# The first group of a causal dynamic convolution and squared-ReLU MLP kernel: turned blocks, raw weight loads, unread products and the third group's first pieces

## The chip, the cores and the metric

The kernel runs on one core of a Trainium2 chip. The core's engines are TensorE (PE in the profile), VectorE (DVE), ScalarE (ACT), GpSimd (POOL) and SyncE (SP), which here issues every transfer; each takes its own instructions in order, and semaphores tie them together. The metric is the device time of one execution in microseconds (us), the median of three runs.

## The reference

```python
# _attn_ref: x is 4 x 4096 x 192, weight_gen 4 x 4096 x 8 heads x 7 taps
w = weight_gen - np.max(weight_gen, axis=-1, keepdims=True)
w = np.exp(w)
w = w / (np.sum(w, axis=-1, keepdims=True) + 1e-09)
pad = K - 1
x_pad = np.concatenate([np.zeros((B, pad, D), dtype=np.float32), x], axis=1)
idx = np.arange(S)[:, None] + np.arange(K)[None, :]
x_unf = x_pad[:, idx, :]
x_unf = x_unf.reshape(B, S, K, H, group)
out = np.einsum('bshk,bskhg->bshg', w, x_unf)
# _moe_ref: w_in is 192 x 2048, w_out 2048 x 192, s and b scalars
h = x @ w_in
r = np.maximum(h, 0.0)
g = s * (r * r) + b
return (g @ w_out).astype(np.float32)
```

A softmax over seven taps weights, for each token and each head of 24 channels, the token and the six before it; the 16384 rows of 192 channels that come out go through an MLP of width 2048. The two weight matrices arrive in double precision; the kernel reads them as pairs of 32-bit words.

## The kernel before

**Tiling.** The tokens are cut into 32 groups of 512. The width of 2048 is cut into four quads of 512, and each quad into two chunks of 256: eight chunks, numbered 0 to 7. Products that must be exact to float32 are made from a high and a low part of each operand: xa and xb hold the high and low parts of the first 128 and the other 64 channels, `wc` of a chunk those of w_in and w_out, gh and gl those of the hidden layer.

**The raw words.** `load_weights(k)` fetches two chunks of w_in and w_out into one tile `r`: four loads of 32 partitions (L183), eight small ones for the channels beyond 32 of each block of 48, called tails here (L194), then w_out by chunk (L201). `convert(i)` turns chunk i into `wc` in four steps that the program places one at a time with `ahead`: the absolute value on ACT (L215); the bits of the high part on DVE (L218 to L226); the high part's cast on ACT (L231) and the low word on DVE (L233, L237); six matmuls and a cast that make the low part (L247 to L250).

**The first group** goes chunk by chunk in the loop at L682, beside the conversion: the first product (`mm1_pair`, L512 and L518), relu and square on ACT (`relu2`, L548 to L554, the last being gh), gl on DVE (`low_g`, L572), the second product of the chunk before (`mm2_pair`, L599). Between them stand pieces of the second group's convolution (`run_pieces(1, ...)`: softmax L297 to L314 with the exponent L305 on ACT, products L329, sums L340 and after). The first group's own convolution (`first_pieces`) is in another layout: x in one tile of 128 partitions, products L411, sums L422 and L433, then 16 matmuls that turn the blocks (`turn`, L446), a cast for the high part (L454) and a difference for the low part (L459). At the last chunk `column_sums` adds the columns of w_out on PE (L274) into a PSUM tile, and `set_bias` reads it on DVE (L282, L283).

**The other groups** run by quads in the loop at L709 (`mm1_quad` L537, `mm2_quad` L617), with the convolution of the group after next to them, `scale` (L629, L635) and `store` (L645 to L654; the last group's are at L651).

**What sets the order.** The program order is the order of each engine (`manual_schedule`); nothing reorders it. Tiles of one tag in a pool take turns in their buffers, so a write waits for the readers of the tile before. SP issues all transfers in order, and their completions go round eight semaphores: the issue of a transfer waits until the transfer eight places before it has landed.

## Time and profile before

| | us |
|---|---|
| median of three runs | 1170.17 |
| lowest and highest of them | 1169.68, 1171.65 |
| the profiled execution | 1168.92 |
| its span, first to last instruction | 1167.2 |
| PE busy in the span | 1138.5 (98%) |
| DVE busy | 937.7 (80%) |
| ACT busy | 824.0 (71%) |

The profile is of one execution. Busy time is summed over an engine's instructions; an idle stretch is put down to what ended it. A microsecond of DVE, ACT or DMA matters only where the engine that sets the end waits for it, so the waits of PE and the chain that ended last are read ahead of the shares.

### The profile page before, as it was taken

Reading aid. Unit: us, or ns where it says so; the run is one execution under the profiler, and the core shown is the slowest. Engines: PE = TensorE matmul, PEld = TensorE weight load, DVE = VectorE, ACT = ScalarE, POOL = GpSimd, SP = SyncE. Lnnn points to the kernel's source line nnn. Section 1 sums busy time; section 2 is a strip of 40 time slices with the busy share of each in tenths; the row PEclk is TensorE's granted clock in tenths of the full one; section 3 lists DMA queues with packets and bytes.
Section 4 is the critical chain, followed back from the end, with each engine's and each line's share of the span. In section 5 each row is a group of like instructions: output and inputs, shape, how many; then the busy total and the mean of one; then the engine's idle time right before and its main releaser. Section 6 shows DMA issues by size and latency. Waiting matters only on the chain.

```text
span 1167.2 us, 29890 instructions
## 1 busy us (share of the span) xinstructions
PE 1138.5 (98%) x12688; PEld 1033.1 (89%) x12688; DVE 937.7 (80%) x1354; ACT 824.0 (71%) x887; POOL 6.2 (1%) x24
## 2 busy tenths in 40 slices
PE   2999999999999999999999999999999999999998
PEld 2688999999999999999999999999999999999997
DVE  7888887788987777887778888778898777888854
ACT  2767767777677677676776776777767777777674
POOL 0000000000000000000000000000000000000000
PEclk9999999999999999999999999999999999999999
DMA  6421222221122221122222122222112222212110
GB/s 159 122 44 29 39 46 47 33 47 25 37 47 47 36 44 33 33 43 47 46 33 47 25 37 46 47 33 46 28 34 46 47 38 42 35 35 39 24 24 14
DMA packets 171145, 50.35 MB, mean 43 GB/s; under 512 B 160196, under 2 KB 163908, under 8 KB 171012
## 3 DMA queue, kind: packets, MB, share of 16 engines
q1 hardware_dynamic: 171012, 48.45, 22.2%
q8 instruction: 99, 1.62, 0.6%
q14 instruction: 34, 0.28, 0.1%
HBM read 27.70 MB, written 12.58 MB: 35 GB/s over the span
## 4 chain that ended last, share of the span: by engine, by line
PE 96%; DVE 2%; DMA 1%; SPq 0%; ACT 0%; issue 0%
PE po L617 48%; PE ph L537 43%; PE po L599 2%; PE ph L512 1%; PE ph L247 1%; PE ph L518 1%; DMA x<-in_x_dram 0%; DVE pr L422 0%; PE ph L446 0%; DVE gl L572 0%; SPq L194 0%; PE ph L274 0%; ACT gh L554 0%; PE ph L249 0%; PE ph L248 0%
## 5 line engine op out<-in xcount | busy, mean ns | idle before, releaser
L617 PE MATMUL po<-wc,gh 64*128 64x384 f32 x3936 | 575.8, 355 | 0.0
L617 PE MATMUL po<-wc,gl 64*128 64x192 f32 x3936 | 475.9, 249 | 0.9 <-DVE gl L572 0.9
L572 DVE TENSOR_TENSOR gl<-r,gh 128x1024 fp32r<-128x1024 f32 x256 | 312.9, 1222 | 199.8 <-ACT gh L554 194.4
L548 ACT ACTIVATE r<-ph 128x1024 f32<-128x1024 f32 x254 | 247.1, 1023 | 290.4 <-PE ph L537 283.8
L617 PEld LDWEIGHTS po<-wc,gl 64*128 64x128 f32 x3936 | 373.3, 187 | 5.9 <-DVE gl L572 1.1
L617 PEld LDWEIGHTS po<-wc,gh 64*128 64x128 f32 x3936 | 369.2, 184 | 4.8
L537 PE MATMUL ph<-xa,wc 64*128 64x512 f32 x2976 | 359.4, 387 | 0.0
L537 PEld LDWEIGHTS ph<-xa,wc 64*128 64x128 f32 x2976 | 278.2, 185 | 50.4 <-issue 0.2
L554 ACT CAST gh<-r 128x1024 fp32r<-128x1024 f32 x254 | 267.1, 1051 | 7.8
L550 ACT ACTIVATE r<-r 128x1024 f32<-128x1024 f32 x254 | 268.6, 1058 | 0.3
L537 PE MATMUL ph<-xb,wc 64*128 64x512 f32 x1488 | 189.0, 386 | 0.0
L329 DVE TENSOR_TENSOR pr<-xt,w 128x1536 f32<-128x1536 f32 (+1 forms) x124 | 187.5, 1553 | 1.4 <-DVE w L314 0.2
L537 PEld LDWEIGHTS ph<-xb,wc 64*128 64x128 f32 x1488 | 139.6, 184 | 29.1
L340 DVE TENSOR_TENSOR pr<-pr 128x1536 f32<-128x1536 f32 (+1 forms) x124 | 140.7, 1155 | 2.1
L629 DVE SCALAR_TENSOR_TENSOR u<-po,s_sb,bias 128x192 f32<-128x192 f32 x128 | 49.7, 409 | 2.1 <-PE po L599 2.1
L635 DVE SCALAR_TENSOR_TENSOR y<-po,s_sb,u 128x192 f32<-128x192 f32 x128 | 49.7, 408 | 0.1
L348 DVE TENSOR_TENSOR acc<-pr 128x768 f32<-128x768 f32 x31 | 29.7, 958 | 1.1
L247 PE MATMUL ph<-r,eye_f 128*128 128x384 f32 x32 | 15.4, 566 | 15.3 <-DVE r L226 15.3
L359 DVE STREAM_TRANSPOSE xT<-acc 128x128 f32<-128x128 f32 x124 | 27.6, 280 | 1.0
L364 DVE STREAM_TRANSPOSE xT<-acc 128x128 f32<-128x128 f32 x124 | 26.3, 269 | 0.0
L599 PE MATMUL po<-wc,gh 128*128 128x384 f32 x80 | 23.7, 361 | 0.0
L247 PEld LDWEIGHTS ph<-r,eye_f 128*128 128x128 f32 x32 | 5.8, 204 | 18.1 <-issue 18.1
(59 smaller groups left out, 360.5 us busy)
## 6 DMA issues: line engine op xcount, KB each, us to landing
xt<-in_x_dram SPq DMA_DIRECT2D x120, 132.0 KB, 3.4
out_dram<-y SPq DMA_DIRECT2D x124, 96.0 KB, 1.9
xb<-xb SPq DMA_DIRECT2D x124, 64.0 KB, 2.3
wg<-in_weight_gen_dram SPq DMA_DIRECT2D x124, 28.0 KB, 2.6
r<-in_moe_w_out_dram SPq DMA_DIRECT2D x8, 384.0 KB, 3.6
r<-in_moe_w_in_dram SPq DMA_DIRECT2D x12, 128.0 KB, 2.6
x<-in_x_dram SPq DMA_DIRECT2D x1, 960.0 KB, 5.3
r<-in_moe_w_in_dram SPq DMA_DIRECT2D x24, 32.0 KB, 1.9
```

What stands on the lines that cost most here:

```text
L247: nc.tensor.matmul(out=o, lhsT=eye_f, rhs=fv[:, c], start=True, stop=False)
L329: nc.vector.tensor_tensor(out=pr[:, k0:k1, :, h * G:(h + 1) * G], in0=bass.AP(xs.tensor, xs.offset, [xs.ap[0], [FQ, n], [FQ, J], [1, G]]), ...
L340: nc.vector.tensor_tensor(out=pr[:, o:o + n], in0=pr[:, o:o + n], in1=pr[:, a:a + n], op=ALU.add)
L537: nc.tensor.matmul(out=h_t[n, p][:, j], lhsT=w1(2 * k + p, part, block, j, rows), rhs=v[rows], start=(at < 2 and c == 0), stop=(at >= 4 an ...
L548: nc.scalar.activation(out=r[p], in_=h_t.pop((n, p)), func=AF.Relu)
L550: nc.scalar.activation(out=r[p], in_=r[p], func=AF.Square)
L554: nc.scalar.copy(out=gh, in_=r[p])
L572: nc.vector.tensor_tensor(out=gl, in0=sq, in1=gh.bitcast(F32), op=ALU.subtract)
L599: nc.tensor.matmul(**m)
L617: nc.tensor.matmul(**m)
L629: nc.vector.scalar_tensor_tensor(out=u[i], in0=o_t[g][tiles[i]][:, 1, :], scalar=s_sb, in1=bias, op0=ALU.mult, op1=ALU.add,)
L635: nc.vector.scalar_tensor_tensor(out=y[:, t], in0=o_t[g][t][:, 0, :], scalar=s_sb, in1=u[i - 1], op0=ALU.mult, op1=ALU.add,)
```

## The change

The change has six parts. The first group's x is loaded in two transfers, cut after the seventh token's words of each partition. The raw words of w_in come in one transfer a chunk, of 128 partitions, in place of four of 32 for one or two chunks; w_out's chunk follows it directly, ahead of the tails, on the same queue. The blocks are turned into two PSUM tiles, h1 and one of the output tiles, in place of the two halves of h0, so the output tiles are now whole banks. `keep_warm` issues seven and, later, four matmuls on x0 whose result nobody reads. For chunk 0 the low cast of chunk 1 stands ahead of the square, and gl ahead of the second group's softmax. And at the last chunk the third group's softmax and first product stand ahead of gl and of `set_bias`; the pieces and `scale` in the next two quads are cut accordingly.

```diff
@@ -138,10 +138,11 @@
             in_=wgf[t0:t0 + T].rearrange("(p t) n -> p (t n)", t=NT),
         )
         src = xf[t0 - HALO:t0 - HALO + 1, 0:1]
-        nc.sync.dma_start(
-            out=x0.rearrange("p t d -> p (t d)"),
-            in_=bass.AP(src.tensor, src.offset, [[NT * D, P], [1, (NT + HALO) * D]]),
-        )
+        for a, b in ((0, K * D), (K * D, (NT + HALO) * D)):
+            nc.sync.dma_start(
+                out=x0.rearrange("p t d -> p (t d)")[:, a:b],
+                in_=bass.AP(src.tensor, src.offset + a, [[NT * D, P], [1, b - a]]),
+            )
         xt_t[0], wg_t[0] = x0, wg
 
     def zeros_before(i):
@@ -170,38 +171,45 @@
     w_in_u = w_in.bitcast(U32)
     w_out_u = w_out.bitcast(U32)
 
-    def load_weights(k, chunks=(slice(0, 2),)):
+    def raw_tile(k):
 
         if k not in raw_t:
             raw_t[k] = raw.tile([P, 2, CW, 2], U32, tag="r", name="r")
-        rw = raw_t[k].rearrange("p c n w -> p c (n w)")
-        for cs in chunks:
-            n = cs.stop - cs.start
-            c0 = (k * QUAD + cs.start * 2) * P * 2
-            src = w_in_u[0:1, c0:c0 + 1]
-            for q in range(Q):
+        return raw_t[k].rearrange("p c n w -> p c (n w)")
+
+    def load_chunk(i):
+
+        k, c = divmod(i, 2)
+        rw = raw_tile(k)
+        src = w_in_u[0:1, i * 4 * P:i * 4 * P + 1]
+        nc.sync.dma_start(
+            out=rw[:, c, CA * 2:CB * 2],
+            in_=bass.AP(src.tensor, src.offset, [[FQ * F * 2, Q], [F * 2, 32], [1, 4 * P]]),
+        )
+        src = w_out_u[i * 2 * P:i * 2 * P + 1, 0:1]
+        nc.sync.dma_start(
+            out=rw[:, c, CO * 2:].rearrange("p (j n) -> p j n", j=2),
+            in_=bass.AP(src.tensor, src.offset, [[D * 2, P], [P * D * 2, 2], [1, D * 2]]),
+        )
+
+    def load_tails(k, c0, n):
+
+        rw = raw_tile(k)
+        for q in range(Q):
+            for i in range(2):
+                f = (q + 2 * i) % Q * FQ + 32
+                c = (k * QUAD + c0 * 2 + 1 - q // 2) * P * 2
+                src = w_in_u[f:f + 1, c:c + 1]
                 nc.sync.dma_start(
-                    out=rw[q * 32:(q + 1) * 32, cs, CA * 2:CB * 2],
-                    in_=bass.AP(
-                        src.tensor, src.offset + q * FQ * F * 2, [[F * 2, 32], [2 * P * 2, n], [1, 2 * P * 2]]
-                    ),
-                )
-            for q in range(Q):
-                for i in range(2):
-                    f = (q + 2 * i) % Q * FQ + 32
-                    c = c0 + (1 - q // 2) * P * 2
-                    src = w_in_u[f:f + 1, c:c + 1]
-                    nc.sync.dma_start(
-                        out=rw[q * 32 + i * TAIL:q * 32 + (i + 1) * TAIL, cs, CB * 2:CO * 2],
-                        in_=bass.AP(src.tensor, src.offset, [[F * 2, TAIL], [2 * P * 2, n], [1, P * 2]]),
-                    )
-            for c in range(cs.start, cs.stop):
-                o = (k * 2 + c) * 2 * P
-                src = w_out_u[o:o + 1, 0:1]
-                nc.sync.dma_start(
-                    out=rw[:, c, CO * 2:].rearrange("p (j n) -> p j n", j=2),
-                    in_=bass.AP(src.tensor, src.offset, [[D * 2, P], [P * D * 2, 2], [1, D * 2]]),
-                )
+                    out=rw[q * 32 + i * TAIL:q * 32 + (i + 1) * TAIL, c0:c0 + n, CB * 2:CO * 2],
+                    in_=bass.AP(src.tensor, src.offset, [[F * 2, TAIL], [2 * P * 2, n], [1, P * 2]]),
+                )
+
+    def load_weights(k):
+
+        for i in (2 * k, 2 * k + 1):
+            load_chunk(i)
+        load_tails(k, 0, 2)
 
     def convert(i):
 
@@ -440,24 +448,25 @@
 
         def turn():
             pr = st["v"]
-            st["ph"] = ph = ps_h.tile([P, 2, T], F32, tag="h0", name="ph")
+            ph = ps_h.tile([P, 2, T], F32, tag="h1", name="ph")
+            st["ph"] = ph[:, 0], ps_o.tile([P, T], F32, tag="o0", name="po")
             for a in range(2):
                 for t in range(NT):
                     nc.tensor.matmul(
-                        out=ph[:, a, t * P:(t + 1) * P], lhsT=pr[:, 3 + a, t * P:(t + 1) * P], rhs=eye_f,
+                        out=st["ph"][a][:, t * P:(t + 1) * P], lhsT=pr[:, 3 + a, t * P:(t + 1) * P], rhs=eye_f,
                         start=True, stop=True,
                     )
 
         def split_hi():
             st["x"] = x = [xtp.tile([P, 2, T], F32R, tag=n, name=n) for n in ("xa", "xb")]
             for h in range(2):
-                nc.scalar.copy(out=x[h][:, 0], in_=st["ph"][:, h])
+                nc.scalar.copy(out=x[h][:, 0], in_=st["ph"][h])
 
         def split_lo():
             x = st["x"]
             for h in range(2):
                 nc.vector.tensor_tensor(
-                    out=x[h][:, 1], in0=st["ph"][:, h], in1=x[h][:, 0].bitcast(F32), op=ALU.subtract
+                    out=x[h][:, 1], in0=st["ph"][h], in1=x[h][:, 0].bitcast(F32), op=ALU.subtract
                 )
             x_t[0] = [[(0, v[:, 0]), (1, v[:, 0]), (0, v[:, 1])] for v in x]
 
@@ -466,6 +475,13 @@
             add(0, 3, 2), add(2, 5), add(2, 6), add(0, 1), last_add,
             turn, split_hi, split_lo,
         ]
+
+    def keep_warm(n):
+
+        o = ps_o.tile([P, T], F32, tag="o1", name="po")
+        x0 = xt_t[0].rearrange("p t d -> p (t d)")[:, 0:2 * D]
+        for _ in range(n):
+            nc.tensor.matmul(out=o[:, 0:2 * D], lhsT=eye_f, rhs=x0, start=True, stop=True)
 
     pieces_t = {}
 
@@ -541,14 +557,16 @@
             if at < 2:
                 hand_over(h_t[n, at])
 
-    def relu2(n, ps=(0, 1), between=None):
+    def relu2(n, ps=(0, 1), between=None, early=False):
         r = {}
         for p in ps:
             r[p] = act.tile([P, 2, T], F32, tag="r", name="r")
             nc.scalar.activation(out=r[p], in_=h_t.pop((n, p)), func=AF.Relu)
         for p in ps:
+            if between and early:
+                between()
             nc.scalar.activation(out=r[p], in_=r[p], func=AF.Square)
-            if between:
+            if between and not early:
                 between()
             gh = gp.tile([P, 2, T], F32R, tag="gh", name="gh")
             nc.scalar.copy(out=gh, in_=r[p])
@@ -573,7 +591,8 @@
         g_t[n, p] = gh, gl
 
     def outputs(g):
-        o_t[g] = [ps_o.tile([P, 2, D], F32, tag=f"o{t}", name="po") for t in range(NT)]
+        banks = [ps_o.tile([P, T], F32, tag=f"o{t}", name="po") for t in range(NT)]
+        o_t[g] = [o[:, 0:2 * D].rearrange("p (a d) -> p a d", a=2) for o in banks]
         y_t[g] = yp.tile([P, NT, D], F32, tag="y", name="y")
 
     def second(n, p, j, t, part, rows=slice(0, P)):
@@ -656,7 +675,9 @@
     with tc.manual_schedule():
         load_first()
         constants()
-        load_weights(0, (slice(0, 1), slice(1, 2)))
+        for i in range(2):
+            load_chunk(i)
+            load_tails(0, i, 1)
         load(1)
         load_weights(1)
         nc.sync.dma_start(out=s_sb, in_=s.partition_broadcast(P))
@@ -669,10 +690,11 @@
                 next(parts[i])
 
         run_pieces(0, 0, 2)
+        keep_warm(7)
         ahead(0, 1)
-        run_pieces(0, 2, 5)
-        run_pieces(0, 5, 7)
+        run_pieces(0, 2, 7)
         ahead(0, 3)
+        keep_warm(4)
         ahead(1, 1)
         run_pieces(0, 7, 14)
         ahead(1, 1)
@@ -685,7 +707,7 @@
             if i == 0:
                 ahead(1, 1)
                 ahead(2, 1)
-            relu2(n, [p], lambda: ahead(i + 1, 1))
+            relu2(n, [p], lambda: ahead(i + 1, 1), i == 0)
             if i == 0:
                 run_pieces(1, 0, 2)
             ahead(i + 2, 2)
@@ -694,8 +716,13 @@
                 sums = column_sums()
             if i > 0:
                 mm2_pair((i - 1) // 2, (i - 1) % 2)
+            if i == 0:
+                low_g(n, p)
             run_pieces(1, *beside[i])
-            low_g(n, p)
+            if i == NC - 1:
+                run_pieces(2, 0, 4)
+            if i > 0:
+                low_g(n, p)
             if i == 0:
                 load_weights(2)
             if i == NC - 1:
@@ -704,7 +731,7 @@
                 load_weights(3)
             if i == 4:
                 load(2)
-        run_pieces(2, 0, 3)
+        run_pieces(2, 4, 5)
         last = NG * NQ - 1
         for n in range(NQ, last + 1):
             g, k = divmod(n, NQ)
@@ -723,10 +750,13 @@
             else:
                 mm2_quad(n - 1)
             a = (3, 5), (5, 8), (9, 14), (0, 2)
-            run_pieces(g + 1 + k // 3, *a[k])
+            a = {NQ: (5, 7), NQ + 1: (7, 8)}.get(n, a[k])
+            run_pieces(g + 1 + k // 3, *a)
+            if n == NQ:
+                scale(g - 1, (0, 2))
             low_g(n, 0)
             if k == 0:
-                scale(g - 1, (0, 2, 1, 3))
+                scale(g - 1, (1, 3) if n == NQ else (0, 2, 1, 3))
                 store(g - 1, 0, NT)
             low_g(n, 1)
             a = (5, 5), (8, 9), (14, 15), (2, 3)
```

**SP, the raw words of chunks 2 and 3.** The rows are transfers by line, written tile and shape; `r` is the tile of raw words, DMAHW0 to DMAHW7 are the eight completion semaphores. Before (the first two loads of 32 partitions stand just ahead):

```order
L183 DMA r<-in_moe_w_in_dram 32x2x512 [waits DMAHW6_49]
L183 DMA r<-in_moe_w_in_dram 32x2x512 [waits DMAHW7_49]
L194 DMA r<-in_moe_w_in_dram 16x2x256 [waits DMAHW0_49]
L194 DMA r<-in_moe_w_in_dram 16x2x256 [waits DMAHW1_49]
L194 DMA r<-in_moe_w_in_dram 16x2x256 [waits DMAHW2_49]
L194 DMA r<-in_moe_w_in_dram 16x2x256 [waits DMAHW3_49]
L194 DMA r<-in_moe_w_in_dram 16x2x256 [waits DMAHW4_49]
L194 DMA r<-in_moe_w_in_dram 16x2x256 [waits DMAHW5_49]
L194 DMA r<-in_moe_w_in_dram 16x2x256 [waits DMAHW6_49]
L194 DMA r<-in_moe_w_in_dram 16x2x256 [waits DMAHW7_49]
L201 DMA r<-in_moe_w_out_dram 128x2x384 [waits DMAHW0_49]
L201 DMA r<-in_moe_w_out_dram 128x2x384 [waits DMAHW1_49]
```

Now:

```order
L185 DMA r<-in_moe_w_in_dram 128x1x512 [waits DMAHW7_49]
L190 DMA r<-in_moe_w_out_dram 128x2x384 [waits DMAHW0_49]
L185 DMA r<-in_moe_w_in_dram 128x1x512 [waits DMAHW1_49]
L190 DMA r<-in_moe_w_out_dram 128x2x384 [waits DMAHW2_49]
L203 DMA r<-in_moe_w_in_dram 16x2x256 [waits DMAHW3_49]
L203 DMA r<-in_moe_w_in_dram 16x2x256 [waits DMAHW4_49]
L203 DMA r<-in_moe_w_in_dram 16x2x256 [waits DMAHW5_49]
L203 DMA r<-in_moe_w_in_dram 16x2x256 [waits DMAHW6_49]
L203 DMA r<-in_moe_w_in_dram 16x2x256 [waits DMAHW7_49]
L203 DMA r<-in_moe_w_in_dram 16x2x256 [waits DMAHW0_49]
L203 DMA r<-in_moe_w_in_dram 16x2x256 [waits DMAHW1_49]
L203 DMA r<-in_moe_w_in_dram 16x2x256 [waits DMAHW2_49]
```

Two loads of 128 partitions, each with w_out behind it, now stand ahead of the tails; before, w_out came after them. The last tail waited for DMAHW7, that of the fourth w_in load; it now waits for the semaphore of the second w_out.

**ACT, the first chunk.** The absolute value (of chunk 2's raw words), relu, square, low cast of chunk 1 (`wc_105`), gh and the exponent. Before:

```order
L215 ACTIVATE t<-r 128x768
L548 ACTIVATE r<-ph 128x1024
L550 ACTIVATE r<-r 128x1024
L250 CAST wc_105<-ph 128x768
L554 CAST gh<-r 128x1024
L305 ACTIVATE e<-e 128x224
```

Now:

```order
L223 ACTIVATE t<-r 128x768
L564 ACTIVATE r<-ph 128x1024
L258 CAST wc_105<-ph 128x768
L568 ACTIVATE r<-r 128x1024
L572 CAST gh<-r 128x1024
L313 ACTIVATE e<-e 128x224
```

The low cast of chunk 1 and the square have changed places; the absolute value of chunk 2 stands ahead of the relu in both.

**DVE, the end of the first group.** Low parts of xb and xa of the second group, gl of the last chunk, the two reads of the column sums (`cs`, `bias`), and the third group's softmax and products. Before:

```order
L377 TENSOR_TENSOR xb<-xT,xb 128x512
L377 TENSOR_TENSOR xa<-xT,xa 128x512
L572 TENSOR_TENSOR gl<-r,gh 128x1024
L282 TENSOR_SCALAR cs<-ph,b_sb 128x192
L283 SCALAR_TENSOR_TENSOR bias<-ph,b_sb,cs 128x192
L297 TENSOR_REDUCE mx<-wg 128x32
L299 TENSOR_TENSOR e<-wg,mx 128x224
L310 TENSOR_REDUCE sm<-e 128x32
L311 TENSOR_SCALAR sm<-sm 128x32
L312 RECIPROCAL sm<-sm 128x32
L314 TENSOR_TENSOR w<-e,sm 128x224
L329 TENSOR_TENSOR pr<-xt,w 128x64x24 x2
```

Now:

```order
L385 TENSOR_TENSOR xb<-xT,xb 128x512
L385 TENSOR_TENSOR xa<-xT,xa 128x512
L305 TENSOR_REDUCE mx<-wg 128x32
L307 TENSOR_TENSOR e<-wg,mx 128x224
L318 TENSOR_REDUCE sm<-e 128x32
L319 TENSOR_SCALAR sm<-sm 128x32
L320 RECIPROCAL sm<-sm 128x32
L322 TENSOR_TENSOR w<-e,sm 128x224
L337 TENSOR_TENSOR pr<-xt,w 128x64x24
L590 TENSOR_TENSOR gl<-r,gh 128x1024
L290 TENSOR_SCALAR cs<-ph,b_sb 128x192
L291 SCALAR_TENSOR_TENSOR bias<-ph,b_sb,cs 128x192
```

The softmax and one product, which stood behind the reads of the column sums, stand ahead of gl and of these reads.

## Rows read from the trace of the kernel before

**Rows 1.** The page: the chain that ended last; the first weight product.

```profile
PE 96%; DVE 2%; DMA 1%; SPq 0%; ACT 0%; issue 0%
...
L247 PE MATMUL ph<-r,eye_f 128*128 128x384 f32 x32 | 15.4, 566 | 15.3 <-DVE r L226 15.3
```

**Rows 2.** Waits of PE, 0 to 130 us: total, times, longest.

```profile
PE ph L446 <- DVE pr L433: 2.9, 1, 2.9
PE ph L512 <- DVE xb L459: 2.6, 1, 2.6
...
PE po L617 <- DVE gl L572: 0.9, 1, 0.9
```

**Rows 3.** Stretches: length, busy time by engine, granted clock, DMA share, GB/s.

```profile
21.90:25.30 3.40, 3.36 (x16) 3.37 (x16) 2.71 (x6) 0.00 (x0) 0.00 (x0) 0.50 1.04 225
...
28.70:32.10 3.40, 3.40 (x12) 1.81 (x10) 3.04 (x6) 0.91 (x1) 0.00 (x0) 0.50 0.40 135
...
33.05:40.00 6.95, 6.30 (x27) 3.80 (x25) 4.46 (x8) 6.77 (x10) 0.00 (x0) 1.00 0.37 108
...
100.00:1167.00 1067.00, 1061.63 (x12260) 973.62 (x12258) 855.14 (x1237) 764.96 (x821) 5.32 (x16) 1.00 0.21 38
```

**Rows 4.** Timeline, DVE and PE at chunk 3: start, duration, line, tiles.

```profile
53.53 1.22 DVE L572 TENSOR_TENSOR gl<-r,gh 128x1024 fp32r<-128x1024 f32 x1
...
54.80 0.36 PE L599 MATMUL po<-wc,gl 128*128 128x192 f32 x1
```

**Rows 5.** Timeline, PE: the first product of chunk 0 and of chunk 2.

```profile
28.14 2.42 PE L512 MATMUL ph<-xa,wc 128*128 128x512 f32 x6 [2.58 <-DVE xb L459]
...
43.10 1.56 PE L512 MATMUL ph<-xa,wc 128*128 128x512 f32 x6
```

**Rows 6.** The page: transfers, size of one, median us to landing.

```profile
xt<-in_x_dram SPq DMA_DIRECT2D x120, 132.0 KB, 3.4
...
x<-in_x_dram SPq DMA_DIRECT2D x1, 960.0 KB, 5.3
r<-in_moe_w_in_dram SPq DMA_DIRECT2D x24, 32.0 KB, 1.9
```

**Rows 7.** Timeline, ACT: chunk 2's absolute value, chunk 0's relu.

```profile
29.49 0.91 ACT L215 ACTIVATE t<-r 128x768 f32<-128x768 f32 x1 [2.03 <-DVE v L237]
32.18 1.02 ACT L548 ACTIVATE r<-ph 128x1024 f32<-128x1024 f32 x1 [1.78 <-PE ph L518]
```

**Rows 8.** Stretches as in rows 3: the x load, the last stores.

```profile
3.50:5.00 1.50, 0.00 (x0) 0.00 (x0) 0.97 (x4) 0.39 (x1) 0.00 (x0) 1.00 1.01 420
...
1162.00:1165.00 3.00, 0.00 (x0) 0.00 (x0) 0.50 (x2) 0.00 (x0) 0.00 (x0) 1.00 0.27 87
```

**Rows 9.** Timeline, SP: the second group's x loads are issued.

```profile
18.13 2.30 SPq L125 DMA_DIRECT2D xt<-in_x_dram  x4
```

**Rows 10.** Timeline, DVE: from chunk 2's conversion to chunk 3's.

```profile
33.21 0.96 DVE L237 SCALAR_TENSOR_TENSOR v<-r,t 128x768 fp32r<-128x768 uint32 x1
36.48 0.39 DVE L310 TENSOR_REDUCE sm<-e 128x32 f32<-128x224 f32 x1 [2.31 <-ACT e L305]
...
37.93 1.76 DVE L329 TENSOR_TENSOR pr<-xt,w 128x1536 f32<-128x1536 f32 x1
39.61 1.22 DVE L572 TENSOR_TENSOR gl<-r,gh 128x1024 fp32r<-128x1024 f32 x1
40.74 0.55 DVE L218 TENSOR_SCALAR t<-t 128x768 f32<-128x768 f32 x1
```

**Rows 11.** Timeline, all engines: the end of the first group.

```profile
82.12 1.05 ACT L554 CAST gh<-r 128x1024 fp32r<-128x1024 f32 x1
...
83.20 1.22 DVE L572 TENSOR_TENSOR gl<-r,gh 128x1024 fp32r<-128x1024 f32 x1 [3.64 <-ACT gh L554]
...
84.34 0.41 DVE L282 TENSOR_SCALAR cs<-ph,b_sb 128x192 f32<-128x192 f32 x1
...
85.10 3.03 PE L537 MATMUL ph<-xa,wc 64*128 64x512 f32 x24
...
85.96 0.39 ACT L305 ACTIVATE e<-e 128x224 f32<-128x224 f32 x1 [2.79 <-DVE e L299]
```

## The prediction

> **What bounds the kernel now.** I read the chain that ended last first. Its row says that PE holds 96% of the span [rows 1], so a microsecond counts only where PE stands still, or where it will after the change. The list of PE's waits says where that is. Three of its rows bear on the change: the blocks of the first group wait 2.9 us for DVE (L446), the first product of the MLP 2.6 us for the last low part (L512 after L459), and L617 0.9 us for a low part of g at the end of the first group [rows 2]. The stretches come next: from 100 us to the end PE is busy in all but half a percent of the time at a granted clock of 1.00, and the list of waits has nothing there, so whatever the first 90 us lose or gain passes one for one to the end [rows 3]. The rest of the reading asks what sets the pace of those 90 us. There PE and DVE are tied: in the fourth chunk DVE ends gl at 53.53 + 1.22 = 54.75, and PE's product with it starts at 54.80 [rows 4]. A delay of DVE in that stage is a delay of PE.
>
> The clock is the last thing to see. In the two stretches that follow the waits of 2.9 and 2.6 us the granted clock was 0.50, the lower of the two levels; after 33.05 us it is 1.00 [rows 3]. The same six matmuls of L512 took 2.42 us there and 1.56 us later [rows 5], so a stretch of 3.4 us at the lower level, as both were, costs 3.4 x (1 - 1.56/2.42) = 1.2 us.
>
> **The front: x in two loads, turned blocks in two tiles, eleven unread products.** The x load took 5.3 us [rows 6]; the second part is 576 of 1920 words, so the first product starts at most 30% of that, 1.6 us, earlier. The separate tiles take the second half of the turning out of the wait for xa: up to the 2.6 us of that wait go. The unread products are of the size of L247, 0.57 us each [rows 1]. Seven take 4.0 us inside the 15.3 us that PE waits for the first conversion, and are free. Four more take 2.3 us of the wait of 2.9; if the blocks are ready sooner than I think, they hold PE up to 2.3 us. What they may buy is the higher clock, up to 2 x 1.2 us. All of this makes the first product of the MLP early, by 2 to 5 us. It is not what is late next.
>
> **What is late next: the raw words of chunks 2 and 3.** ACT takes its work in order, and L215 of chunk 2 stands ahead of the relu of chunk 0; before, it ran at 29.49 and the relu at 32.18 [rows 7]. Queued behind it now are that relu, the low cast of chunk 1, the square, gh and the exponent of the second group's weights; DVE's gl and conversion and PE's second product wait for them. L215 needs the last of eight tails. Eight semaphores go round, so each transfer's issue waits until the one eight places before it has landed. With one w_in load a chunk and w_out ahead of the tails, the fifth to eighth tails wait for w_in 2, w_out 2, w_in 3 and w_out 3.
>
> How long do these take? The source of the new w_in load has 4 as its slowest dimension. The nearest row is that of the last stores (L651), whose destination has 4 there too: the share of the 16 DMA engines was 0.27, four of 16, at 87 GB/s, where the x load had all of them and 420 [rows 8]. So I take 256 KB (262 thousand bytes) at 87 GB/s, 3.0 us; the best that four engines can do by the x load's row is 420/4 = 105 GB/s, 2.5 us. The 393 thousand bytes of w_out take 0.9 us at 420. They are behind one another on those four engines: 2 x (3.0 + 0.9) = 7.8 us. They begin when the second group's x is through. Its loads are issued by 18.13 + 2.30 = 20.43 [rows 9] and land 3.4 us later [rows 6]: 23.8. So w_out 3 lands at 31.6, the eighth tail is issued then and lands after 1.9 [rows 6], at 33.5, and L215 runs at 33.6 where it ran at 29.49: 4.1 us late.
>
> That row is of a store, this is a load. The Trainium skill ("DMA: Bandwidth & Descriptors", section "Why a DMA increments its semaphore by 16 and not by 1") says that the number of engines is the largest up to 16 that divides the slowest dimension of both sides, and it makes no difference between loads and stores. By that rule this load has four; the trace of before agrees for the store with its 0.27. Were it sixteen, the sum would be that of the first rival.
>
> From there by DVE and ACT. Relu at 33.6 + 0.9 = 34.5 (L215 takes 0.91); relu 1.02, the low cast some 0.8, square and gh some 1.05 each: gh is there at 38.4. DVE's conversion of chunk 2 ended at 33.21 + 0.96 = 34.17, 4.7 after L215 began, so now at 38.3 [rows 7, 10]. Then gl, moved ahead of the pieces, 1.22 (39.6); the softmax of the second group, 37.93 - 36.48 = 1.45 (41.05); its first product, 39.61 - 37.93 = 1.68 (42.7). Chunk 3's conversion starts there; before it started at 40.74 [rows 10]. That is **+2.0 us** in a chain without slack [rows 4]. Moving gl ahead of the pieces takes away PE's 0.9 at 40 us, but it does not shorten DVE's row of work, and the row is what counts. The ends: with 2.5 us a load, +1.0; with a last tail that takes as long as the x loads (3.4 for 1.9), +3.5. Less than nothing is the first rival.
>
> **The end of the first group: the third group's pieces ahead of the last low part.** PE's seventh matmul of the next group's first product (at wc_105) writes the tile that holds the column sums, so it waits for set_bias, two reads on DVE. Before, gl(7) started at 83.20, right behind gh (82.12 + 1.05), took 1.14 and was followed by the reads, 84.34 to 85.2; PE came to that matmul at 85.10 + 6 x 0.126 = 85.86 and did not wait [rows 11]. Now DVE runs the maximum and difference (in its idle 3.64 us, free), then waits for the exponent, which stands behind gh on ACT: 83.17 + 0.39 = 83.56. Then softmax 1.45, the product 1.68, gl 1.14, the reads 2 x 0.41 [rows 10, 11]: 88.65. PE waits 88.65 - 85.86 = **+2.8 us**. Behind that matmul on PE stand all later ones, so nothing covers it. What is bought is the wait of 0.9 at L617 [rows 2], since DVE has less to do behind set_bias: **-0.9**. Both ends are narrow (exponent overlapping gh, -0.1).
>
> A wait of 2.8 us is as long as the two (2.9 and 2.6) that were followed by the lower clock [rows 2, 3]. I take one stretch of it, **+1.2**, at 5 in 7; without it the sum is 1.2 less. The pieces and the scale that are cut differently in the fifth and sixth quads move DVE work within a stretch where PE had no waits [rows 3]; I put them at nothing, since PE would have to wait there first.
>
> **Sum.** +2.0 + 2.8 - 0.9 + 1.2 = +5.1 on the profiled 1168.92: 1174.0. The profiled run is 1.25 below the median of three, 1170.17, so the median becomes 1175.3. Ends of the forecast: +1.0 + 2.8 - 0.9 = +2.9 (1173.1) and +3.5 + 2.8 + 1.2 = +7.5 (1177.7).
>
> **Rivals.** *Sixteen engines.* If the w_in load is spread after all, chunks 2 and 3 (1.5 MB) take some 3.7 us at 420 GB/s from 23.8, and with the tail L215 runs at about 29.4, as before. Then the early first product counts: relu at 30.2, gh at 34.1, DVE 34.2 + 1.22 + 1.45 + 1.68 = 38.55 instead of 40.74, -2.2. With the end of the group, -2.2 + 2.8 - 0.9 = -0.3, or +0.9 with the clock: 1169.9 to 1171.1, no change. For it: the tile's side has 128 partitions, and no load of this shape is in the trace; against it, the store's row. *The front carries.* Before, L215 of chunk 2 was released by DVE, not by a transfer [rows 7]; it waited for the conversion behind the turned blocks. Those come earlier by up to the 1.6 us of the x load and part of the 2.6 us of PE's wait, some 3 us in all, and if the words of chunks 2 and 3 are in by then, L215 goes at 26.5 and DVE gains 2.2 + 3 = 5.2: -5.2 + 2.8 - 0.9 = -3.3, 1166.9. It is faster by over 0.2% from a gain of 4.2 on, with L215 at 27.3 or sooner. Against it: even sixteen engines bring the words only at about 29, by the reckoning above, unless SP's issues move up by 2 us. *Four engines, but PE keeps its clock* is the forecast less 1.2: 1174.1.
>
> **How the numbers follow.** What a measurement of this kernel can tell from no change is about 0.2%, 2.3 us: 1167.8 to 1172.5. The forecast has 0.74 (0.53 with the lower clock, 0.21 without, all of it slower). Sixteen engines has 0.18, of which 0.15 is within and 0.03, with less gained at the front, slower. The front carries has 0.08, faster. So faster 0.08, same 0.15, slower 0.77. The range reaches down to the first rival's lower end, 1170.0, and up to the forecast's upper end, rounded up, 1178.0; outside are the second rival and some 0.08 above.
>
> **What would show it.** In the changed kernel's trace: the w_in load alone on the queue at a DMA share near 0.25 and some 3 us; L223 (the old L215) of chunk 2 at 33 to 34, released by a DMA; chunk 3's conversion on DVE at 42 to 43; a wait of PE at L553 for DVE L291 of 2.5 to 3 us near 88, and a granted clock of 0.5 behind it; no wait at L636. I am wrong if L223 of chunk 2 runs by 30, if the wait at L553 is under 1.5 us, or if PE shows a slack to DVE in the middle chunks that takes up the 2.0.

## The result and the profile after

The changed kernel takes 1176.47 us (median of six runs, 1175.98 to 1177.29) where the kernel before takes 1170.31 beside it: ratio 1.0051, 95% interval 1.0038 to 1.0064, slower by 6.2 us. The profiled execution took 1176.62 us with a span of 1174.9, against 1168.92 and 1167.2: 7.7 us more, which the trace has to account for. Each column of the table is one execution; that of before lies 1.4 us under the median of its kernel, that of after 0.15 above.

| start, us | before | after | later by |
|---|---|---|---|
| SP: x loads of the second group | 18.13 | 20.77 | 2.64 |
| ACT: absolute value of chunk 2 | 29.49 | 36.20 | 6.71 |
| DVE: conversion of chunk 3 | 40.74 | 45.03 | 4.29 |
| ACT: relu of chunk 7 | 79.97 | 84.32 | 4.35 |
| PE: first quad of the next group | 85.10 | 89.46 | 4.36 |
| PE: second quad | 91.88 | 100.80 | 8.92 |
| PE: third quad | 101.86 | 109.57 | 7.71 |

After the third quad nothing is gained or lost. So there are three places: 4.36 us by the first quad, 8.92 - 4.36 = 4.56 between it and the second, and 1.21 given back by the third.

The waits of PE over the whole span (total, times, longest) answer to [rows 2]:

```profile
PE ph L528 <- ACT r L564: 8.1, 1, 8.1
...
PE ph L553 <- DVE bias L291: 2.7, 1, 2.7
PE ph L528 <- DVE xa L468: 0.8, 1, 0.8
```

The 2.9 at the turned blocks and the 0.9 at the third group's second product are gone, and of the 2.6 at the first product of the MLP 0.8 is left. The second chunk's product (L528) now waits 8.1 us for the relu of chunk 0, and the next group's first product (L553) 2.7 us for the second read of the column sums. Why the relu is late stands on ACT (timeline: start, duration, line, idle before and its releaser; answers to [rows 7]):

```profile
36.20 0.89 ACT L223 ACTIVATE t<-r 128x768 f32<-128x768 f32 x1 [10.36 <-DMA r<-in_moe_w_in_dram]
36.99 1.01 ACT L564 ACTIVATE r<-ph 128x1024 f32<-128x1024 f32 x1
```

ACT stood idle for 10.4 us until a tail of w_in had landed, with the relu behind it. SP's timeline shows what the tails themselves waited for; the four rows of L203 are the fifth to eighth tails of chunks 2 and 3, each issued when w_in 2, w_out 2, w_in 3 and w_out 3 had landed (answers to [rows 9]):

```profile
20.77 2.29 SPq L125 DMA_DIRECT2D xt<-in_x_dram  x4
...
29.82 0.31 SPq L203 DMA_DIRECT2D r<-in_moe_w_in_dram  x1
...
30.76 0.31 SPq L203 DMA_DIRECT2D r<-in_moe_w_in_dram  x1
...
33.33 0.31 SPq L203 DMA_DIRECT2D r<-in_moe_w_in_dram  x1
...
34.26 0.31 SPq L203 DMA_DIRECT2D r<-in_moe_w_in_dram  x1
```

From w_out 2 to w_in 3 there are 2.57 us, from w_in 2 to w_out 2 and from w_in 3 to w_out 3 0.94 and 0.93. In a stretch between, with the w_in load almost alone, the DMA share was 0.26 (last but one number; the clock stands ahead of it), as for the last stores in [rows 8]:

```profile
32.00:33.00 1.00, 0.00 (x0) 0.00 (x0) 0.00 (x0) 0.00 (x0) 0.00 (x0) 0.98 0.26 97
```

Behind the wait of 8.1 us PE's granted clock was 0.50. This did not add to the delay: DVE, whose row of work the chunks follow, had no gap from chunk 2's conversion (37.12) to chunk 3's (45.03).

```profile
38.00:42.00 4.00, 3.95 (x10) 2.53 (x12) 3.90 (x6) 3.97 (x6) 0.00 (x0) 0.50 0.85 209
```

The end of the first group, all engines (answers to [rows 11]):

```profile
87.43 0.38 ACT L313 ACTIVATE e<-e 128x224 f32<-128x224 f32 x1
87.84 0.39 DVE L318 TENSOR_REDUCE sm<-e 128x32 f32<-128x224 f32 x1 [3.21 <-ACT e L313]
...
89.29 1.76 DVE L337 TENSOR_TENSOR pr<-xt,w 128x1536 f32<-128x1536 f32 x1
89.46 0.96 PE L553 MATMUL ph<-xa,wc 64*128 64x512 f32 x6
90.97 1.22 DVE L590 TENSOR_TENSOR gl<-r,gh 128x1024 fp32r<-128x1024 f32 x1
92.10 0.41 DVE L290 TENSOR_SCALAR cs<-ph,b_sb 128x192 f32<-128x192 f32 x1
92.55 0.42 DVE L291 SCALAR_TENSOR_TENSOR bias<-ph,b_sb,cs 128x192 f32<-128x192 f32 x1
...
93.12 3.14 PE L553 MATMUL ph<-xa,wc 64*128 64x512 f32 x18 [2.70 <-DVE bias L291]
```

Softmax, product, gl and the reads stand in a row, and PE, after six matmuls, waits for the last of them. In the stretches behind that wait (granted clock third from the end) the clock is at its lower level, 0.50, from 95 to 97, and back at 1.00 from about 98.5; the first two rows mix both levels:

```profile
93.00:96.50 3.50, 3.38 (x22) 3.19 (x24) 3.50 (x3) 0.00 (x0) 0.00 (x0) 0.70 0.03 5
96.50:98.50 2.00, 2.00 (x13) 1.54 (x10) 0.67 (x1) 0.93 (x2) 0.00 (x0) 0.67 0.00 0
98.50:100.80 2.30, 2.30 (x16) 2.14 (x16) 0.88 (x3) 2.27 (x4) 0.00 (x0) 1.00 0.00 0
...
95.00:97.00 2.00, 2.00 (x12) 1.84 (x12) 2.00 (x2) 0.00 (x0) 0.00 (x0) 0.50 0.04 8
```

4.56 - 2.70 = 1.86 us is therefore what follows the wait in this execution. Most of it is the clock, but not all: with the same wait and no lower clock behind it (128 rows, pieces alone) the time between the two quads is still 0.25 us longer than before and the wait together.

### The profile page after: what moved, and what is told of

Read it like the earlier page. It is cut to its first block, busy times and chain, and to the rows that moved or that the text cites. A ratio compares the mean times of both kernels' runs of the same rounds, so it can differ in the third digit from the quotient of the medians.

```text
span 1174.9 us, 29916 instructions
## 1 busy us (share of the span) xinstructions
PE 1148.4 (98%) x12710; PEld 1039.3 (88%) x12710; DVE 938.0 (80%) x1354; ACT 823.6 (70%) x887; POOL 6.1 (1%) x24
## 4 chain that ended last, share of the span: by engine, by line
PE 96%; DMA 2%; SPq 1%; DVE 0%; ACT 0%; issue 0%; ACTq 0%
PE po L636 48%; PE ph L553 43%; DMA r<-in_moe_w_out_dram 2%; PE po L618 2%; PE ph L528 1%; PE ph L255 1%; PE ph L534 1%; SPq L105 0%; SPq L185 0%; SPq L125 0%; PE ph L257 0%; PE ph L256 0%; ACT r L564 0%; DVE pr L337 0%; DMA r<-in_moe_w_in_dram 0%
## 5 line engine op out<-in xcount | busy, mean ns | idle before, releaser
L553 PE MATMUL ph<-xa,wc 64*128 64x512 f32 x2976 | 360.4, 388 | 2.7 <-DVE bias L291 2.7
L553 PEld LDWEIGHTS ph<-xa,wc 64*128 64x128 f32 x2976 | 279.3, 185 | 52.9 <-issue 3.4
L553 PE MATMUL ph<-xb,wc 64*128 64x512 f32 x1488 | 189.9, 388 | 0.0
L553 PEld LDWEIGHTS ph<-xb,wc 64*128 64x128 f32 x1488 | 140.8, 185 | 28.9
L367 DVE STREAM_TRANSPOSE xT<-acc 128x128 f32<-128x128 f32 x124 | 27.6, 280 | 1.0
L223 ACT ACTIVATE t<-r 128x768 f32<-128x768 f32 x8 | 7.3, 908 | 23.0 <-DMA r<-in_moe_w_in_dram 23.0
L528 PE MATMUL ph<-xa,wc 128*128 128x512 f32 x48 | 14.6, 439 | 8.9 <-ACT r L564 8.1
```

What stands on the lines that cost most here:

```text
L553: nc.tensor.matmul(out=h_t[n, p][:, j], lhsT=w1(2 * k + p, part, block, j, rows), rhs=v[rows], start=(at < 2 and c == 0), stop=(at >= 4 an ...
```

## The experiments

Every time is set against the kernel before on the same chip in the same session; those medians lie between 1169.58 and 1170.48, so differences from them are compared, not times. The rows come from the profiled execution of each, and one row varies between executions of the same code: "pieces alone" has the code of before up to the last chunk, and there SP issues the second group's x 1.15 us later and the relu of chunk 7 runs 1.48 us later.

| kernel | median | against before | ratio, interval | x loads on SP | abs. of chunk 2 | conversion of chunk 3 | relu of chunk 7 | wait for the reads |
|---|---|---|---|---|---|---|---|---|
| before | | | | 18.13 | 29.49 | 40.74 | 79.97 | none |
| changed | 1176.47 | +6.2 | 1.0051 (1.0038 to 1.0064) | 20.77 | 36.20 | 45.03 | 84.32 | 2.7 |
| 128 rows | 1168.51 | -1.1 | 0.9989 (0.9979 to 0.9998) | 16.57 | 28.05 | 36.89 | 76.10 | 2.7 |
| four loads | 1171.65 | +2.1 | 1.0019 (1.0010 to 1.0029) | 18.59 | 31.20 | 40.04 | 79.25 | 2.7 |
| pieces back | 1173.31 | +3.7 | 1.0028 (1.0017 to 1.0039) | 20.40 | 36.69 | 45.52 | 84.76 | none |
| both | 1168.20 | -1.4 | 0.9987 (0.9978 to 0.9997) | 18.48 | 31.41 | 40.25 | 79.41 | none |
| pieces alone | 1172.48 | +2.8 | 1.0022 (1.0013 to 1.0032) | 19.28 | 30.66 | 42.23 | 81.45 | 2.7 |
| loads alone | 1173.76 | +4.0 | 1.0032 (1.0021 to 1.0043) | 20.08 | 35.51 | 44.61 | 85.13 | none |
| loads, pieces back | 1167.05 | -2.6 | 0.9977 (0.9968 to 0.9987) | 18.40 | 30.38 | 39.20 | 78.36 | none |
| no unread products | 1167.31 | -2.4 | 0.9975 (0.9966 to 0.9985) | 18.99 | 30.44 | 39.44 | 78.59 | none |
| exponent early | 1167.13 | -2.6 | 0.9976 (0.9967 to 0.9986) | 18.64 | 30.32 | 39.16 | 78.30 | none |
| scale cut | 1166.33 | -3.5 | 0.9966 (0.9954 to 0.9978) | 18.26 | 29.91 | 38.74 | 77.96 | none |
| first two split | 1175.47 | +5.7 | 1.0044 (1.0029 to 1.0059) | 19.17 | 35.01 | 43.84 | 83.07 | 2.7 |
| turn back | 1167.32 | -3.2 | 0.9973 (0.9962 to 0.9984) | 18.18 | 29.82 | 40.21 | 79.43 | none |

**128 rows: the four DMA engines.**

```diff
-            in_=bass.AP(src.tensor, src.offset, [[FQ * F * 2, Q], [F * 2, 32], [1, 4 * P]]),
+            in_=bass.AP(src.tensor, src.offset, [[F * 2, P], [1, 4 * P]]),
```

> The changed kernel, but each one-transfer load of w_in reads 128 rows that follow one another in place of four blocks of 32 rows, 48 apart: the source's slowest dimension is 128 and not 4, all else alike (shape in the tile, bytes, place in the queue). The weights are therefore taken from other rows, so part of the computation is changed. Theory A (the load runs on four DMA engines because of the 4, and that makes the raw words late): the DMA share during a load is near 1, the absolute value of chunk 2 (L223) runs at 28 to 30 in place of 36.2, the relu of chunk 7 (L564) at 78 to 79 in place of 84.3, and the time is 5 to 6.5 us below the changed kernel: 1170 to 1171.5. Theory B (the tails come late because they stand behind w_out in the rotation of eight semaphores): L223 of chunk 2 stays at 34 to 36 and the time within 1.5 us of the changed kernel's 1176.5.

With nothing changed but the addresses, the time fell by 7.3 us, counted from the kernel before of each session, further than theory A said. A stretch in the loads of chunks 2 and 3 and the two rows on ACT:

```profile
23.00:25.00 2.00, 1.44 (x6) 0.67 (x4) 1.97 (x5) 1.25 (x2) 0.00 (x0) 1.00 1.02 372
```

```profile
28.05 0.89 ACT L223 ACTIVATE t<-r 128x768 f32<-128x768 f32 x1 [3.80 <-DMA r<-in_moe_w_in_dram]
28.84 1.01 ACT L564 ACTIVATE r<-ph 128x1024 f32<-128x1024 f32 x1
```

A share of 1.02 at 372 GB/s in place of 0.26 at 97: the 4 in the address pattern is the cause, and theory B falls. One thing that made the gain larger than expected is that SP reached the second group's x loads at 16.57, ahead of the kernel before. In the profiled run the 2.7 us wait for the reads was also not followed by a lower clock, but that run lies 1.7 us below the median of its kernel, and what the clock did behind the wait in the others is not on record; so this does not account for the median.

**Four loads.**

```diff
-        nc.sync.dma_start(
-            out=rw[:, c, CA * 2:CB * 2],
-            in_=bass.AP(src.tensor, src.offset, [[FQ * F * 2, Q], [F * 2, 32], [1, 4 * P]]),
-        )
+        for q in range(Q):
+            nc.sync.dma_start(
+                out=rw[q * 32:(q + 1) * 32, c, CA * 2:CB * 2],
+                in_=bass.AP(src.tensor, src.offset + q * FQ * F * 2, [[F * 2, 32], [1, 4 * P]]),
+            )
```

> The changed kernel with four loads of 32 partitions for each chunk of w_in, in the place of the one of 128; w_out stays ahead of the tails. Theory A (four engines): as with consecutive rows, less what three more issues a chunk cost on SP (3 x 0.45 us): L223 of chunk 2 at 30 to 31.5, time 1170.5 to 1172.5. Theory B (the order of tails and w_out): L223 of chunk 2 at 33 or later, time above 1174.

Theory A, inside its numbers: 31.20 and 1171.65. Four loads in place of one give back 4.1 us (6.2 less 2.1). Chunk 2's absolute value is still 0.8 us later than with the loads as before (30.38). The order of tails and w_out or the greater number of issues may cost that; the runs do not part the two, and 0.8 is no more than one execution can differ from another.

**Pieces back, and both.**

```diff
-            if i == NC - 1:
-                run_pieces(2, 0, 4)
...
-        run_pieces(2, 4, 5)
+        run_pieces(2, 0, 3)
...
-            a = {NQ: (5, 7), NQ + 1: (7, 8)}.get(n, a[k])
...
-            if n == NQ:
-                scale(g - 1, (0, 2))
```

> The changed kernel with the third group's first pieces back behind the last low part and the two reads of the column sums, as before the change; the loads stay as changed. Theory A (the wait at L553 is due to these pieces alone, and the lower clock behind it to the wait): no wait of PE for L291, no granted clock below 0.95 after 80 us, a wait of about 0.9 at L636 is back, and the time is 2.7 + 1.9 - 0.9 = 3.5 us below the changed kernel: 1172.5 to 1173.5. Rival (the stage before is so late that another wait takes the place of this one): less than 1.5 us below.

> Both undone: four loads of 32 partitions for each chunk of w_in, and the third group's pieces back; x in two loads, the turned blocks in two tiles, the unread products, gl ahead of the softmax and w_out ahead of the tails stay. Theory A says that the two are independent and what is left is a gain at the front: 1170.5 to 1172.5 less 3.5, that is 1167 to 1169, 1 to 3 us below the kernel before (1170.3). Rival (the front carries nothing to the end because DVE's row of work in the chunks sets the pace): 1170 to 1171.5.

Both came as theory A said: 1173.31, with the wait for the reads gone, the clock at 1.00 from 84 us to 100 and the 0.9 back; and 1168.20 with both undone. By the differences from before, undoing the pieces gives back 2.5 us on the changed kernel, where 3.5 was expected, and 3.5 on the kernel with four loads; alone they cost 2.8, below. These agree within about a microsecond, so the two parts add up as far as the times can tell. The clock with the pieces back, and the wait:

```profile
84.00:100.00 16.00, 16.00 (x120) 13.82 (x120) 10.09 (x17) 9.48 (x10) 0.00 (x0) 1.00 0.38 58
```

```profile
PE po L636 <- DVE gl L590: 0.9, 1, 0.9
```

**Each part alone on the kernel before.** The first is the reverse of the diff above; the second takes over only the loads (w_in in one load a chunk, w_out ahead of the tails).

> The kernel before with one part of the change: the third group's softmax and first product ahead of the last low part and the reads of the column sums (and the pieces and the scale of the next two quads as in the change). Theory A (the wait costs by itself what it cost in the changed kernel): a wait of PE at L537-like line for the second read of 2.7 to 2.9 us, the wait of 0.9 at the third group's second product gone: +1.9, and with one stretch of the lower clock behind it +3.1 to +3.7; against a kernel before of 1169.6 that is 1171.5 without and 1172.7 to 1173.3 with the lower clock. In the run with 128 consecutive rows the same wait was not followed by the lower clock, in the one with four loads it was; which of the two comes here is open. Rival (the pieces cost only where the raw words are late): within 0.7 us of the kernel before.

> The kernel before with one part of the change: the raw words by chunk, w_in in one load of 128 partitions, w_out behind it and ahead of the tails. Theory A (this part alone makes the absolute value of chunk 2 late and the whole of the delay hangs on it): L223-like line of chunk 2 at 35 to 37, released by a DMA, the relu of chunk 7 at 84 to 85 in place of 79.97, and 4 to 5.5 us above the kernel before: 1173.7 to 1175.2. Rival (the delay needs the other parts too, the early x or the unread products): under 2.5 us above.

The loads alone cost 4.0 us, at the lower end of theory A, and the rival falls. The pieces alone cost 2.8 by the median, between the two cases of theory A; its rival falls too. In the profiled run the wait is there in full and the clock does not fall behind it (that run's relu of chunk 7 is 1.48 us later than before; where the median's share beyond 1.9 comes from is not settled). The line of waits and the stretch behind it:

```profile
PE ph L537 <- DVE bias L283: 2.7, 1, 2.7
```

```profile
90.24:96.30 6.06, 6.06 (x46) 5.31 (x46) 4.91 (x6) 2.97 (x4) 0.00 (x0) 1.00 0.01 3
```

**Loads and pieces back; no unread products; the exponent early.** The first undoes both parts with the loads of before; the second also drops the two calls; the third adds this to the first:

```diff
-            relu2(n, [p], lambda: ahead(i + 1, 1), i == 0)
+            if i == NC - 1:
+                run_pieces(2, 0, 1)
+                relu2(n, [p], lambda: run_pieces(2, 1, 2), True)
...
+            if i == NC - 1:
+                run_pieces(2, 2, 3)
```

> The changed kernel with the raw words loaded wholly as before (four loads of 32 partitions for two chunks, tails, w_out last) and the third group's pieces back: what is left is x in two loads, the turned blocks in two tiles, the unread products, and gl ahead of the softmax. Theory A (chunk 3's conversion begins some 8.8 us after chunk 2's absolute value; that one is set by the landing of the raw words): the absolute value at 28.5 to 29.5, chunk 3's conversion on DVE at 37.3 to 38.3 where it was at 40.25 with four loads a chunk, and the time 1 to 3 us below that kernel: 1165.5 to 1167.5. Rival (w_out ahead of the tails is no loss): the time of four loads a chunk, 1168.2, within 0.7.

> The same kernel without the eleven unread products. Theory A (the first product of the MLP is early anyway, and the relu waits for the raw words through ACT's order): the granted clock falls to 0.5 in one or two stretches before 35 us, and the time changes by less than 0.7 us against the kernel with them. Rival (the clock is what they buy): 1.2 to 2.4 us slower.

> The kernel with loads and pieces back, and one step added: the third group's exponent stands between the relu and the square of the last chunk, and its softmax ahead of the last low part, so that both run in DVE's idle 3.6 us; the products stay behind the reads of the column sums. Theory A (the pieces hurt only because the exponent stands behind gh and the product follows it): no wait of PE at the first product of the next group, the wait of 0.9 at the third group's second product gone, 0.5 to 0.9 us faster than without the step. Rival (what DVE does earlier there is not what the second product waits for): within 0.4 us.

The first is 2.6 us faster than the kernel before, in the range expected: this is what the front of the change is worth with the loads and pieces as before. Its rows are later than expected, 30.38 for the absolute value of chunk 2 where 28.5 to 29.5 was said and 39.20 for chunk 3's conversion where 37.3 to 38.3 was.

The unread products buy nothing that the times show: 0.3 us between the two, intervals over one another. On PE they did what they were put in for. With them, then without, the matmuls that turn the blocks and the first product:

```profile
22.18 1.13 PE L448 MATMUL ph<-eye_f,pr 128*128 128x128 f32 x8 [0.34 <-DVE pr L434]
...
25.49 1.21 PE L521 MATMUL ph<-xa,wc 128*128 128x512 f32 x4 [0.78 <-DVE xa L461]
26.63 0.96 PE L527 MATMUL ph<-xb,wc 64*128 64x512 f32 x6
```

```profile
23.00 2.05 PE L448 MATMUL ph<-eye_f,pr 128*128 128x128 f32 x8 [2.58 <-DVE pr L434]
...
26.41 2.73 PE L521 MATMUL ph<-xa,wc 128*128 128x512 f32 x6
29.07 0.96 PE L527 MATMUL ph<-xb,wc 64*128 64x512 f32 x6
```

Without them the first product took about as long as at a granted clock of 0.50 in [rows 5] (2.42, against 1.56 at 1.00) and ended at 30.0 in place of 27.6. That is still ahead of the relu (31.24 and 31.17), so nothing comes of it in time. The granted clock of the two runs seems to say the reverse; the stretch from 16 to 20 us with them, then without:

```profile
16.00:20.00 4.00, 4.00 (x11) 2.38 (x10) 3.97 (x4) 0.95 (x3) 0.00 (x0) 0.66 0.74 130
```

```profile
16.00:20.00 4.00, 3.76 (x8) 2.29 (x8) 3.93 (x5) 0.90 (x1) 0.00 (x0) 1.00 0.70 129
```

The run without them has 1.00 throughout, but the durations of its matmuls contradict that up to some 28 us. Going by the durations, the slower stretch that theory A expected came, and changed nothing in time, as it said.

With the early exponent there was no wait at the reads, as theory A said, but it gave nothing in time, and the wait of 0.9 at the third group's second product stayed: theory A falls there.

**Scale cut.** Of the moved pieces only this:

```diff
+            if n == NQ:
+                scale(g - 1, (0, 2))
             low_g(n, 0)
             if k == 0:
-                scale(g - 1, (0, 2, 1, 3))
+                scale(g - 1, (1, 3) if n == NQ else (0, 2, 1, 3))
```

> The kernel with loads and pieces back (1167.05), and of the moved pieces only the scale of the second group's quad in two halves, one ahead of each low part. Theory A (the wait of 0.9 at the third group's second product is for a low part that stands behind four scaled tiles on DVE, and the cut of the scale is what took it away in the changed kernel, not the softmax that moved): that wait is gone or under 0.2, and the time is 0.6 to 0.9 lower, 1166.1 to 1166.5. Rival (it was DVE's lighter load behind the reads): the wait stays, within 0.3.

The line of waits in the kernel without the cut was the first below; in this one no wait of PE is left behind the chunks, and the time is 1166.33. The third quad starts 8.80 us after the second in place of 9.97.

```profile
PE po L629 <- DVE gl L583: 0.9, 1, 0.9
```

By the medians this is the fastest kernel here: 3.5 us below the kernel before (0.9966, 0.9954 to 0.9978). It is 0.8 below the kernel without the cut, as theory A said. The intervals of the two overlap, so that the cut is what took the wait away is shown by the rows, and its worth in time only roughly.

**First two split.** The four loads of above for chunks 0 and 1 alone (`if i < 2`).

> The changed kernel, but chunks 0 and 1 of w_in come in four loads of 32 partitions each; chunks 2 to 7 stay in one load a chunk. Theory A (of the 6.7 us by which chunk 2's absolute value is late, about 2.6 are SP's: the tails of chunks 0 and 1 wait for the slow loads of these chunks, so the second group's loads and the words of chunks 2 and 3 are issued 2.6 us later): L125 on SP at about 18.2 to 18.6 in place of 20.8, L223 of chunk 2 at 33 to 34 in place of 36.2, the time 2 to 2.7 us below the changed kernel, 1173.8 to 1174.5. Rival (the words of chunks 2 and 3 are slow in themselves): L223 of chunk 2 at 35.5 or later, within 1 us.

```profile
19.17 2.29 SPq L125 DMA_DIRECT2D xt<-in_x_dram  x4
```

```profile
35.01 0.89 ACT L230 ACTIVATE t<-r 128x768 f32<-128x768 f32 x1 [9.87 <-DMA r<-in_moe_w_in_dram]
```

The time is that of the rival, 0.5 to 1.0 us below the changed kernel; the rows lie between the two theories. SP is 1.60 us earlier than in the changed kernel, the absolute value 1.19. With 19.17, SP is back within the 18.1 to 19.3 of the seven profiled runs with the loads of before, so what still makes the absolute value late are the words of chunks 2 and 3 themselves. In the kernels where these come in one slow load each, it stands 13.1 to 14.0 us behind the end of SP's x loads: 36.20 - 23.06 = 13.14 after the change, 35.51 - 22.37 = 13.14 with the loads alone, 35.01 - 21.46 = 13.55 here, 36.69 - 22.69 = 14.00 with the pieces back. With four loads it is 31.20 - 20.88 = 10.32. By these differences the slow loads of chunks 2 and 3 make up 2.8 to 3.7 us of the delay, and SP's lateness some 2.

**Turn back.** The blocks turned into the halves of h0, on the fastest kernel.

```diff
-            ph = ps_h.tile([P, 2, T], F32, tag="h1", name="ph")
-            st["ph"] = ph[:, 0], ps_o.tile([P, T], F32, tag="o0", name="po")
+            ph = ps_h.tile([P, 2, T], F32, tag="h0", name="ph")
+            st["ph"] = ph[:, 0], ph[:, 1]
```

> The kernel with loads and pieces back and the scale cut (1166.33), but the blocks turned into the two halves of one tile, h0, as before the change. Theory A (what the front carries to the end is that the first product of the MLP is done before chunk 2's absolute value, so that the relu follows it at once; the two tiles are what makes it so early): the high part's casts start 1 to 2 us later, the relu of chunk 0 comes 1 us or more after chunk 2's absolute value, and the time is 0.5 to 2 us higher, 1166.8 to 1168.3. Rival (there is slack: the first product ended 1 us or more ahead of the relu, and the early x and the low part of g ahead of the softmax carry the gain): within 0.4 us.

On ACT the absolute value, relu and low cast with two tiles, then with one:

```profile
29.91 0.89 ACT L216 ACTIVATE t<-r 128x768 f32<-128x768 f32 x1 [4.31 <-DMA r<-in_moe_w_out_dram]
30.70 1.01 ACT L557 ACTIVATE r<-ph 128x1024 f32<-128x1024 f32 x1
31.61 0.80 ACT L251 CAST wc<-ph 128x768 fp32r<-128x768 f32 x1
```

```profile
29.82 0.91 ACT L216 ACTIVATE t<-r 128x768 f32<-128x768 f32 x1 [3.75 <-DMA r<-in_moe_w_out_dram]
30.84 1.03 ACT L557 ACTIVATE r<-ph 128x1024 f32<-128x1024 f32 x1
...
33.08 0.80 ACT L251 CAST wc<-ph 128x768 fp32r<-128x768 f32 x1 [1.21 <-PE ph L250]
```

PE's wait for xb, gone with two tiles, is back, and the first product starts at 26.76 in place of 23.95, and runs slower (2.71 us for its six matmuls, against 1.56 at a granted clock of 1.00 in [rows 5]):

```profile
23.95 0.73 PE L521 MATMUL ph<-xa,wc 128*128 128x512 f32 x2
```

```profile
26.76 2.71 PE L521 MATMUL ph<-xa,wc 128*128 128x512 f32 x6 [2.58 <-DVE xb L461]
```

The relu is only 0.14 us later, against theory A, but the low cast of chunk 1 waits for PE, and chunk 3's conversion starts 1.47 us later. In time the difference is 1.0 by the medians and 0.3 against the kernels before of the two sessions, and the intervals overlap: the trace shows the mechanism, the times do not settle its size.

## Why the prediction came out

1176.47 lies 1.2 us above the 1175.3 forecast, in the range and on its side, and the two delays that the forecast named are there. That the number is so near is in part luck. In the trace the terms came to +7.7, where +5.1 was forecast and +7.5 was the upper end. The forecast then added 1.25, since the profiled run of before lay that far below its median; the profiled run of the changed kernel lies 0.15 above its own, and these 1.4 us took back half of the 2.6 that the terms were short. By the steps:

*The front* came as forecast: the first product of the MLP starts at 24.07 in place of 28.14, 4.1 us early where 2 to 5 was said (its last four matmuls at 25.57, behind the wait of 0.8). The unread products were mis-sized. Each is two matmuls in the trace, so seven took 6.23 us and four 2.74, where 4.0 and 2.3 were taken; the seven were free all the same, since PE stood idle for 3.15 us behind them. The higher clock that they might buy came at the first product, but was worth nothing in time, as the kernel without them shows.

```profile
6.07 6.23 PE L484 MATMUL po<-x,eye_f 128*128 128x384 f32 x14 [6.07 <-DMA x<-in_x_dram]
15.46 1.29 PE L255 MATMUL ph<-r,eye_f 128*128 128x384 f32 x2 [3.15 <-DMA r<-in_moe_w_out_dram]
...
19.39 2.74 PE L484 MATMUL po<-x,eye_f 128*128 128x384 f32 x8
...
24.07 0.73 PE L528 MATMUL ph<-xa,wc 128*128 128x512 f32 x2
```

*The end of the first group* was right to a tenth: 2.8 expected, 2.70 measured, by the rows it named, and it is 2.7 in all five kernels that keep the pieces and none in the others.

*The w_in load on four engines* was right, and the experiment with 128 rows shows it. The size of a load was a little off: 2.57 us where 3.0 was taken from the store's 87 GB/s and 2.5 was the lower end; w_out took 0.93 for 0.9.

*The size of the delay in the chunks* was the term that failed: +2.0 was forecast, with +3.5 as its upper end, and +4.35 came between the two profiled runs. Some of that is the execution of before that was profiled: against the relu of chunk 7 in "pieces alone" (81.45, the same code up to there) the changed kernel is 2.87 late. By either it is more than 2.0, and by the medians the changed kernel with the pieces back is 3.7 above the kernel before. The failing step is "Its loads are issued by 18.13 + 2.30 = 20.43": SP's order was read from the trace of before as though it stood still. But the loads of chunks 0 and 1 are slow too, and their tails wait for them in the same rotation. SP reached the second group's x at 20.77 (20.1 to 20.8 in the three kernels with these loads), against 18.1 to 19.3 in the seven with the loads of before, and at 19.17 when only chunks 0 and 1 were split. From the end of these issues on the reckoning held: 33.6 - 20.43 = 13.2 forecast, 13.1 to 14.0 measured. From chunk 2's absolute value to chunk 3's conversion 42.7 - 33.6 = 9.1 was forecast and 8.83 measured, and from there to the relu of chunk 7 it is 39.29 against 39.23 before: no slack, as said.

*The wait of 0.9* went, but not for the reason given. It is not DVE's lighter load behind the reads: the early exponent took the softmax out of it and the wait stayed. It is the low part that stood behind four scaled tiles, as the cut of the scale alone shows. The trace puts it at 1.21 with what hangs on it.

*The clock* was put at 1.2 and cost 1.6. The chance was right to be open: of the five profiled runs with a wait of 2.7 us, it fell in three (the changed kernel, four loads, first two split) and not in two (128 rows, pieces alone). From the first to the second quad the three took 11.3 to 11.4 us and the two 9.7, where it was 6.8 before; with 128 rows 9.74 less 6.78 and 2.71 leaves the 0.25 that goes with the wait. The two quads of that run:

```profile
81.22 0.97 PE L553 MATMUL ph<-xa,wc 64*128 64x512 f32 x6
...
90.96 3.02 PE L553 MATMUL ph<-xa,wc 64*128 64x512 f32 x24
```

With these numbers, 4.35 + 2.70 + 1.86 - 1.21 = 7.70, the 7.7 of the spans, with 1.86 for the clock and what goes with the wait.

The first rival was the right one to set up: the kernel with 128 rows is that rival. It came out 1.1 us below the kernel before, where -0.3 to +0.9 was given for it; SP was earlier than that sum had it.

## What to carry to other kernels

Where one transfer takes the place of several, look at the slowest dimension of both of its patterns before counting issues: here a 4 there held the queue at 97 GB/s where it moved 372 without it, and one load in place of four cost 4 us. That 4 stands in the source; the stores of [rows 8] have theirs in the destination, at a share of 0.27. A slow transfer delays not only its reader but the queue that issues it, through the rotation of its semaphores, so the reckoning of its start has to begin at the first such transfer and not at the one that is read late. And work that is moved into an idle stretch must be ready there: the softmax moved ahead of gl waited for an exponent that stood behind gh, and took gl and PE with it. With the exponent early there was no such wait; but that kernel also left the product behind the reads, so the shares of the two are not parted.
